# Overlapping the stages of MOE 1 in a single-core mLSTM and two-MOE kernel, with fewer warm-up products

## The chip, the cores and the metric

The kernel runs on one core of a Trainium2 chip. The metric is the device time of the core in microseconds (us): before the change it is 999.03 us, the median of three runs that lie between 998.11 and 1000.72 us. A core has a tensor engine (PE), a vector engine (DVE), a scalar engine (ACT), a general engine (POOL) and a queue that starts most transfers (SP); each runs its own list of instructions in the order in which it stands, and they wait for each other by semaphores.

## The reference

Three layers follow each other: a recurrent attention over 2 x 8 heads, a first MOE (a plain two-layer network with a piecewise activation), and a second MOE with eight experts whose gates are balanced over all tokens.

```
x = attn_out.transpose(0, 2, 1, 3).reshape(1536, 320)
# MOE 1
h = x @ w_in                       # 1536 x 320 @ 320 x 2048
g = where(h >= 1, h, where(h <= -1, 0, (h + 1) ** 2 / 4))
x = g @ w_out                      # 1536 x 2048 @ 2048 x 320
# MOE 2
P = exp(x @ w_gate - max); 8 times: P /= P.sum(1); P /= P.sum(0); P *= N / E
out = sum over e of P[:, e] * (relu(x @ w1[e]) @ w2[e])
```

## The kernel before

Large products are made in float32 split into a high and a low part, so that one product of the mathematics is eight matmuls of the chip. The tokens stand in twelve tiles of 128. Attention handles one tile after the other (`attn`, lines 370 to 465); its result goes, transposed and split, into `XH` and `XL`, which MOE 1 reads.

MOE 1 runs in five stages (`STAGES`, line 40): tokens 0 to 511 with the first half of the hidden layer, in two parts of 256 columns (stage 0); tokens 512 to 1023 with the first half (stage 1); tokens 1024 to 1535 with both halves (stage 2); then the second half for the first 512 (stage 3) and for the second 512 tokens (stage 4). The loop at line 587 goes over them. For each block of hidden units it makes a *first product* (`gemm_k`, line 131: eight matmuls into one of two PSUM banks named `g1`), an activation (`moe1_act`, lines 552 to 561: three operations on ACT, a maximum on DVE at line 558 that also releases the bank in the stages with 512 columns, a copy on ACT at 559, a subtraction on DVE at 560), and a *weighted sum* (`moe1_g2`, lines 563 to 574: eight matmuls with `w_out`, added up in three banks named `g2`). The sums are held back: `prevs` keeps up to three blocks (two in stage 0), so that a block's activation runs beside the products of the next ones.

At the end of a stage the loop at line 650 empties `prevs`, and only then the stage's accumulated banks are read: stages 0 and 1 copy them to memory (line 657), stages 2 to 4 add what was kept, fold the third bank and split the result into `XH` and `XL` (lines 659 to 666). All stages use the same three `g2` banks.

While stages 0 and 1 run, the loop calls `next(rest)` for pieces of the attention of tiles 2 to 11, and `pump_w` for decoding the weights of MOE 1 from 64-bit floats on ACT and DVE. A scheduler that works through the program at build time decides in which order each engine's instructions stand, so pieces of attention, first products and sums are mixed there.

`warm` (line 307) issues products of zeros that change no result: four ahead of the attention product of line 413 in tiles 2 to 7 (line 410), two ahead of each of the eight first products of stage 0 (line 615), and others at the start. PSUM has eight banks here: two `g1`, three `g2`, two `at` and one `ax`; `at` and `ax` serve attention, and after MOE 1 the gates of MOE 2 (`at`) and the fourth accumulator of MOE 2 (`ax`).

Of the kernel before, what the change touches and what calls it, by code (L numbers as in the profile page):

```python
# [12 lines left out]
ACTF = mybir.ActivationFunctionType  # L13
ALU = mybir.AluOpType
# [26 lines left out]
NPIECE = (9, 12, 18, 18, 18)  # L41
# [8 lines left out]
def mlstm_moe_moe_kernel(  # L50
# [14 lines left out]
    mm = nc.tensor.matmul  # L65
    act = nc.scalar.activation
    vec = nc.vector
# [8 lines left out]
    def bank(tag):  # L76
        n = {"g1": 2, "g2": 3, "at": 2, "ax": 1}[tag]
        return ps.tile([128, 512], F32, name="bk_" + tag, tag=tag, bufs=n)
# [20 lines left out]
    def htile(w, kind):  # L99

        if kind != "gs" and hhome:
            hcount[0] += kind == "hi"
            h = hhome[0][kind == "lo"]
            i = hcount[0] % (h.shape[1] // 512) * 512
            return h[:, i : i + w]
        n = {"gs": NGS, "hi": NHL, "lo": NHL}[kind]
        return pools["hp"].tile([128, 512], F32 if kind == "gs" else F32R, name=kind, tag=kind, bufs=n)[:, :w]
# [11 lines left out]
    def split_x(planes, cols):  # L119
        for k, x in planes:  # L120
            act(out=XH[:, k, cols], in_=x, func=ACTF.Copy)
        for k, x in planes:
            vec.tensor_tensor(out=XL[:, k, cols], in0=x, in1=f(XH[:, k, cols]), op=ALU.subtract)
# [9 lines left out]
    with ExitStack() as atx:  # L133
# [53 lines left out]
        wz = ap.tile([128, 128], mybir.dt.bfloat16, name="wz")  # L187
# [182 lines left out]
        def attn(t, tags):  # L370
# [29 lines left out]
            if not last:  # L400
                gp.tensor_tensor(
                    out=kw.rearrange("p (i r) d -> p r i d", r=2)[:, :, :, 0:40], in0=kk.rearrange("p (i r) d -> p r i d", r=2),
                    in1=G[:, :, 127:128].rearrange("p (r i) d -> p r i d", r=2).to_broadcast([128, 2, 4, 40]), op=ALU.mult,
# [3 lines left out]
                for pr in range(4):  # L407
                    mm(pi[:, pr * 82 : (pr + 1) * 82], qk_t[0:104, 0, pr, :], Cst[:, b, pr, :], start=True, stop=True)
            pa = bank(ta)
            if 2 <= t < 8:  # L410
                warm(WA, pa)
            for h in range(8):
                mm(pa[:, h * 41 : (h + 1) * 41], A[h % 2][:, h // 2, :], vw[:, h, :], start=True, stop=True)  # L413
# [3 lines left out]
            if not last:  # L417
# [6 lines left out]
                if c:  # L424
                    gp.tensor_tensor(
                        out=Cst[:, b, :, :], in0=Cst[:, b, :, :],
                        in1=lend[:, c * 8 + b * 4 : c * 8 + b * 4 + 4].unsqueeze(2).to_broadcast([104, 4, 82]), op=ALU.mult,
                    )
            pav = pa[:, 0:328].rearrange("p (h d) -> p h d", h=8)
            if c:  # L430
                hv = ap.tile([128, 8, 41], F32, name="hv", tag="hv")
                vec.tensor_tensor(
                    out=hv, in0=pi[:, 0:328].rearrange("p (h d) -> p h d", h=8),
# [118 lines left out]
        def moe1_act(pg, early):  # L552
            t, hi, lo = (htile(512, x) for x in ("gs", "hi", "lo"))
            act(out=t, in_=pg, func=ACTF.Relu, scale=-1.0, bias=1.0)  # L554
            act(out=t, in_=t, func=ACTF.Relu, scale=-0.5, bias=1.0)
            act(out=t, in_=t, func=ACTF.Square)  # L556
            g = pg if early else t
            dve_at.append(vec.tensor_tensor(out=g, in0=pg, in1=t, op=ALU.max))  # L558
            act(out=hi, in_=g, func=ACTF.Copy)
            vec.tensor_tensor(out=lo, in0=g, in1=f(hi), op=ALU.subtract)  # L560
            return hi, lo

        def moe1_g2(pp, first, last, f0, w, hi, lo):

            for u in range(512 // w):
                ff, ts = f0 + u, slice(u * w, u * w + w)
                wf = WM[ff // 8][1][:, ff % 8, :]
                st, sp = first, last and u == 512 // w - 1
                for k in range(2):
                    mm(pp[k], wf[:, k * 128 : (k + 1) * 128], hi[:, ts], start=st, stop=False)  # L570
                    mm(pp[k], wf[:, k * 128 : (k + 1) * 128], lo[:, ts], start=False, stop=False)  # L571
                    mm(pp[k], wf[:, 256 + k * 128 : 256 + (k + 1) * 128], hi[:, ts], start=False, stop=sp)  # L572
                mm(pp[2], wf[:, 512:640], hi[:, ts], start=st, stop=False)  # L573
                mm(pp[2], wf[:, 512:640], lo[:, ts], start=False, stop=sp)  # L574
# [9 lines left out]
        held = ap.tile([128, 3, 512], F32, name="held")  # L584
        g0f = G0.rearrange("p h t -> p (h t)")
        held = {0: [held[:, k, :] for k in range(3)], 512: [g0f[:, 0:512], g0f[:, 512:1024], id4]}
        for si, (t0, hfs, w) in enumerate(STAGES):
            nf = 512 // w
            f_last = hfs[-1] * 8 + 7
            pp = [bank("g2") for _ in range(3)]  # L590
            if w < 512:
                for p in pp:
                    mm(p, wz, wz[:, 0:1].to_broadcast([128, 512]), start=True, stop=False)
            prevs = []
            for hf in hfs:
                if si == 2 and hf == 0:

                    hhome[0] = [ap.tile([128, 1536], F32R, name=f"hq{i}", tag=f"qk{i}", bufs=1) for i in range(2)]
                if si == 3:
                    while w_state[0] < 18:  # L600
                        pump_w()
                    rtx.close()
                    rtx = ExitStack()
                    open_right(rtx, hp=1, raw=2, gw=1)
                    wgr = pools["gw"].tile([128, 3, NE], F32, name="wgr")
                    wgs = pools["gw"].tile([128, 5, NE], F32R, name="wgs")
                    wg2 = pools["gw"].tile([128, 2, 2, NE], F32R, name="wg2")
                    hhome.clear()
                for o in range(0, 512, w):
                    while len(done) * 128 < t0 + o + w:  # L610
                        next(rest)
                    for ff in range(hf * 8, hf * 8 + 8, nf):
                        need_w(ff + nf - 1)
                        pg = bank("g1")
                        if w < 512:
                            warm(WG, pg)
                        for u in range(nf):
                            fc = (ff + u) % 8 * 128
                            pe_at = gemm_k(pg[:, u * w : u * w + w], WM[hf][0], slice(fc, fc + 128), slice(t0 + o, t0 + o + w))
                        while len(prevs) >= (LAG2 if w == 512 else LAG1):  # L620
                            moe1_g2(*prevs.pop(0))
                        st = ff == hfs[0] * 8 and w == 512
                        sp = ff + nf - 1 == f_last and o + w == 512
                        prevs.append(([p[:, o : o + w] for p in pp], st, sp, ff, w, *moe1_act(pg, w < 512)))
                        if w_state[0] < NPIECE[si]:
                            if si:
                                with tc.issue_after(dve_at[-2].ins):
                                    pump_w()
                            else:
                                pump_w()  # L630
                        credit += nf * RATE[si]
                        while credit >= 1:
                            if si:

                                with tc.issue_after(pe_at[0].ins), tc.issue_after(dve_at[-3].ins):
                                    next(rest, None)
                            else:
                                next(rest, None)
                            credit -= 1
                        if si == 3 and ff == 12:  # L640
                            nc.sync.dma_start(wgr, w_gate)
                            split_k(wgs, 0, NE, wgr)
                            act(out=wg2.rearrange("p k u e -> p u k e"), in_=f(wgs[:, 0:4, :]).rearrange("p (u k) e -> p u k e", u=2), func=ACTF.Copy)
                            cur, jobs = expert_w(0)
                        if si * 8 + ff % 8 >= 28:
                            next(jobs, None)
            if si == 4:
                for _ in jobs:
                    pass
            for p in prevs:  # L650
                moe1_g2(*p)
            if si < 2:
                if si == 1:
                    for _ in rest:
                        pass
                for k, p in enumerate(pp):
                    act(out=held[t0][k], in_=p, func=ACTF.Copy)
                continue
            if si > 2:
                for k, p in enumerate(pp):  # L660
                    vec.tensor_tensor(out=p, in0=p, in1=held[t0][k], op=ALU.add)
            tr = htile(512, "gs")
            act(out=tr[0:64], in_=pp[2][64:128], func=ACTF.Copy)
            act(out=tr[64:128], in_=pp[2][0:64], func=ACTF.Copy)
            vec.tensor_tensor(out=tr, in0=pp[2], in1=tr, op=ALU.add)
            split_x([(0, pp[0]), (1, pp[1]), (2, tr)], slice(t0, t0 + 512))
        atx.close()


# [156 lines left out]
```

## Time and profile before

| what | value |
|---|---|
| time, median of 3 runs | 999.03 us (998.11 to 1000.72) |
| time of the profiled execution | 997.13 us |
| its span, first to last instruction | 995.1 us |
| PE busy | 978.6 us of the span, 98% |
| DVE busy | 472.1 us, 47% |
| ACT busy | 345.5 us, 35% |
| granted clock of PE | 1.00 of full speed (2.4 GHz) |
| MOE 2 begins | about 296 us after the span's start |

A row of the timeline gives the start, the duration, the engine, the line of the code and what is written and read; in brackets stands how long the engine was idle just before, and what it waited for. A matmul's duration includes its way through the array, and the next one starts before it ends, so the cost of one in a row of many is the distance between two starts. Times count from the start of the span.

### The profile page before, as it was taken

What the parts mean: (1) busy time and instruction counts of PE and PEld (TensorE: products, weight loads), DVE (VectorE), ACT (ScalarE), POOL (GpSimd) and SP (SyncE); (2) the same over time, 40 slices, a digit from 0 to 9 for tenths busy, and PEclk for the clock granted to TensorE, in tenths of its full rate; (3) what the DMA queues carried; (4) which work ended last, traced back from release to release, by engine and by line L of the source; (5) the groups of instructions that cost most, each with busy time, mean ns of one, the idle gap of its engine ahead of it and who ended that gap; (6) DMA issues with size and microseconds to landing.
All of it is one profiled execution on the core that took longest, in us unless ns stands there. A gap on an engine that the chain in (4) does not pass through costs nothing.

```text
span 995.1 us, 13508 instructions
## 1 busy us (share of the span) xinstructions
PE 978.6 (98%) x5520; PEld 860.2 (86%) x5520; DVE 472.1 (47%) x856; ACT 345.5 (35%) x625; POOL 32.2 (3%) x43
## 2 busy tenths in 40 slices
PE   9989999998999999999999999999999999999998
PEld 5778988787788899999999999999999999999997
DVE  9999796864454554322522432242253234222222
ACT  3643455886664223212411321141132113111111
POOL 2212110000000000000000000000000000000000
PEclk9999999999999999999999999999999999999999
DMA  6855430230002001200300210030021002000000
GB/s 171 260 171 164 123 111 2 82 115 2 1 30 88 1 1 58 59 1 2 117 1 1 68 49 1 1 117 1 1 85 34 1 16 72 1 1 1 27 27 27
DMA packets 42190, 51.91 MB, mean 52 GB/s; under 512 B 3360, under 2 KB 35744, under 8 KB 42128
## 3 DMA queue, kind: packets, MB, share of 16 engines
q1 hardware_dynamic: 42128, 51.05, 17.2%
q8 instruction: 43, 0.70, 0.3%
q14 instruction: 19, 0.16, 0.0%
HBM read 49.03 MB, written 2.01 MB: 51 GB/s over the span
## 4 chain that ended last, share of the span: by engine, by line
PE 88%; DVE 8%; ACT 2%; issue 1%; DMA 1%; DVEq 0%
PE bk_g L131 43%; PE bk_g L726 8%; PE bk_g L728 8%; PE bk_g L727 8%; PE bk_ax L727 3%; PE bk_ax L726 3%; PE bk_ax L728 3%; PE bk_g L570 2%; PE bk_g L572 2%; PE bk_g L571 2%; PE bk_at L413 2%; PE bk_at L392 1%; PE bk_g L574 1%; PE bk_g L573 1%; DVE G L396 1%
## 5 line engine op out<-in xcount | busy, mean ns | idle before, releaser
L131 PE MATMUL bk_g<-XH,wk 128*128 128x512 f32 (+1 forms) x1240 | 400.1, 388 | 4.2 <-DVE gs L558 4.2
L746 DVE SCALAR_TENSOR_TENSOR lo<-bk_g,hi 128x512 fp32r<-128x512 f32 x192 | 132.6, 691 | 375.8 <-ACT hi L745 374.9
L131 PE MATMUL bk_g<-XL,wk 128*128 128x512 f32 (+1 forms) x744 | 285.2, 384 | 0.0
L131 PEld LDWEIGHTS bk_g<-XH,wk 128*128 128x128 f32 x1240 | 230.6, 188 | 48.3 <-DVE gs L558 5.8
L745 ACT ACTIVATE hi<-bk_g 128x512 fp32r<-128x512 f32 x192 | 114.4, 596 | 455.0 <-PE bk_g L131 454.6
L726 PE MATMUL bk_g<-wf,hi 128*128 128x320 f32 x576 | 177.4, 308 | 0.0
L727 PE MATMUL bk_g<-wf,hi 128*128 128x320 f32 x576 | 177.0, 307 | 0.0
L728 PE MATMUL bk_g<-wf,lo 128*128 128x320 f32 x576 | 176.9, 308 | 0.0
L131 PEld LDWEIGHTS bk_g<-XL,wk 128*128 128x128 f32 x744 | 140.0, 188 | 21.9 <-issue 0.2
L726 PEld LDWEIGHTS bk_g<-wf,hi 128*128 128x128 f32 x576 | 108.0, 187 | 6.8 <-ACT hi L745 0.2
L727 PEld LDWEIGHTS bk_g<-wf,hi 128*128 128x128 f32 x576 | 108.1, 188 | 6.3
L728 PEld LDWEIGHTS bk_g<-wf,lo 128*128 128x128 f32 x576 | 107.9, 187 | 0.0
L727 PE MATMUL bk_ax<-wf,hi 128*128 128x320 f32 x192 | 59.1, 308 | 0.0
L726 PE MATMUL bk_ax<-wf,hi 128*128 128x320 f32 x192 | 59.0, 307 | 0.0
L728 PE MATMUL bk_ax<-wf,lo 128*128 128x320 f32 x192 | 58.4, 304 | 0.0
L554 ACT ACTIVATE gs<-bk_g 128x512 f32<-128x512 f32 x48 | 28.4, 592 | 36.1 <-PE bk_g L131 35.6
L558 DVE TENSOR_TENSOR gs<-bk_g,gs 128x512 f32<-128x512 f32 x40 | 27.4, 688 | 25.3 <-ACT gs L556 25.2
L760 DVE SCALAR_TENSOR_TENSOR acc<-bk_g,P,acc 128x320 f32<-128x320 f32 x63 | 30.8, 545 | 15.4 <-PE bk_g L728 15.4
L726 PEld LDWEIGHTS bk_ax<-wf,hi 128*128 128x128 f32 x192 | 36.1, 188 | 0.0
L728 PEld LDWEIGHTS bk_ax<-wf,lo 128*128 128x128 f32 x192 | 36.1, 188 | 0.0
L727 PEld LDWEIGHTS bk_ax<-wf,hi 128*128 128x128 f32 x192 | 35.9, 187 | 0.0
L544 DVE TENSOR_TENSOR wf<-raw,wf 128x640 fp32r<-128x640 f32 x32 | 26.4, 825 | 18.9 <-ACT wf L543 18.9
(214 smaller groups left out, 1001.0 us busy)
## 6 DMA issues: line engine op xcount, KB each, us to landing
raw<-in_w_dram SPq DMA_DIRECT2D x32, 320.0 KB
raw<-in_w_dram SPq DMA_DIRECT2D x32, 256.0 KB
kvo_t<-in_kvo_dram SPq DMA_DIRECT2D x12, 484.0 KB
raw<-in_w_out_dram SPq DMA_DIRECT2D x8, 640.0 KB
raw<-in_w_in_dram SPq DMA_DIRECT2D x8, 512.0 KB
raw<-in_w_dram SPq DMA_DIRECT2D x64, 64.0 KB
qk<-in_qk_dram SPq DMA_DIRECT2D x24, 160.0 KB
G<-g_d SPq DMA_DIRECT2D x5, 512.0 KB
```

The source lines that it names most:

```text
L131: return [mm(dst, a, b, start=i == 0, stop=i == len(seq) - 1) for i, (a, b) in enumerate(seq)]
L413: mm(pa[:, h * 41 : (h + 1) * 41], A[h % 2][:, h // 2, :], vw[:, h, :], start=True, stop=True)
L544: vec.tensor_tensor(out=wf[:, fs, 320:640], in0=rs[n], in1=f(wf[:, fs, 0:320]), op=ALU.subtract)
L554: act(out=t, in_=pg, func=ACTF.Relu, scale=-1.0, bias=1.0)
L558: dve_at.append(vec.tensor_tensor(out=g, in0=pg, in1=t, op=ALU.max))
L570: mm(pp[k], wf[:, k * 128 : (k + 1) * 128], hi[:, ts], start=st, stop=False)
L726: mm(pp[i], hi[:, ts], wf[:, ff, 0:320], start=st, stop=False)
L727: mm(pp[i], hi[:, ts], wf[:, ff, 320:640], start=False, stop=False)
L728: mm(pp[i], lo[:, ts], wf[:, ff, 0:320], start=False, stop=sp)
L745: act(out=hi, in_=pg, func=ACTF.Relu)
L746: vec.scalar_tensor_tensor(out=lo, in0=pg, scalar=0.0, in1=f(hi), op0=ALU.max, op1=ALU.subtract)
L760: vec.scalar_tensor_tensor(out=acc[:, t, :], in0=pp[i], scalar=P[:, t, e : e + 1], in1=acc[:, t, :], op0=ALU.mult, op1=ALU.add)
```

## The change

Three things change. First, the list `prevs` now lives across the stages. At the end of a stage it is not emptied: the last sums of a stage (three, two in stage 0) follow the first products of the next stage, one behind each, and the stage's banks are read (`moe1_end`) once its last sum is issued. Only stage 4 empties the list. Second, the accumulators are taken when a stage's first sum is issued, and stages 2 and 4 take the banks `ax`, `at`, `at` where stages 0, 1 and 3 take the three `g2`. The decoding of weights pauses in stage 2 while sums of stage 1 are still held back. Third, `warm` is called ahead of line 413 in tiles 2 to 4 in place of 2 to 7, and in stage 0 ahead of the first four first products in place of all eight: 12 and 8 products of zeros fewer.

```diff
-            if 2 <= t < 8:
+            if 2 <= t < 5:
                 warm(WA, pa)
...
+        prevs, ends = [], []
+        def run_prev():
+            stage, o, w, ff, st, sp, hi, lo = prevs.pop(0)
+            if not stage["pp"]:
+                stage["pp"] = [bank(x) for x in (("ax", "at", "at") if stage["id"][0] in (2, 4) else ("g2",) * 3)]
+                for p in stage["pp"] if w < 512 else ():
+                    mm(p, wz, wz[:, 0:1].to_broadcast([128, 512]), start=True, stop=False)
+            moe1_g2([p[:, o : o + w] for p in stage["pp"]], st, sp, ff, w, hi, lo)
+            if sp:
+                ends.append((*stage["id"], stage["pp"]))
+        def moe1_end(si, t0, pp):
+            if si < 2:
+                for k, p in enumerate(pp):
+                    act(out=held[t0][k], in_=p, func=ACTF.Copy)
+                return
+            if si > 2:
+                for k, p in enumerate(pp):
+                    vec.tensor_tensor(out=p, in0=p, in1=held[t0][k], op=ALU.add)
+            tr = htile(512, "gs")
...
         for si, (t0, hfs, w) in enumerate(STAGES):
...
-            pp = [bank("g2") for _ in range(3)]
-            if w < 512:
-                for p in pp:
-                    mm(p, wz, wz[:, 0:1].to_broadcast([128, 512]), start=True, stop=False)
-            prevs = []
+            stage = {"id": (si, t0), "pp": None}
...
-                        if w < 512:
+                        if w < 512 and o == 0:
                             warm(WG, pg)
...
                         while len(prevs) >= (LAG2 if w == 512 else LAG1):
-                            moe1_g2(*prevs.pop(0))
+                            run_prev()
...
-                        if w_state[0] < NPIECE[si]:
+                        prevs.append((stage, o, w, ff, st, sp, *moe1_act(pg, w < 512)))
+                        while ends:
+                            moe1_end(*ends.pop())
+                        if w_state[0] < NPIECE[si] and (si != 2 or prevs[0][0] is stage):
...
-            for p in prevs:
-                moe1_g2(*p)
...
+        while prevs:
+            run_prev()
+        moe1_end(*ends.pop())
```

On PE, at the border from stage 2 to stage 3, the kernel before has the last sums of stage 2 (lines 570 to 574, accumulators `bk_g2`), and then first products (line 131) into one `g1` bank after the other:

```order
L573 MATMUL bk_g2_1717<-hq0_1718,wf_1744 128x512
L574 MATMUL bk_g2_1717<-hq1_1719,wf_1744 128x512
L131 MATMUL bk_g1_2189<-XH_66,wk_634 128x512
L131 MATMUL bk_g1_2189<-XL_67,wk_634 128x512
L131 MATMUL bk_g1_2189<-XH_66,wk_634 128x512 x2
L131 MATMUL bk_g1_2189<-XL_67,wk_634 128x512
L131 MATMUL bk_g1_2189<-XH_66,wk_634 128x512 x2
L131 MATMUL bk_g1_2189<-XL_67,wk_634 128x512
L131 MATMUL bk_g1_2207<-XH_66,wk_634 128x512
L131 MATMUL bk_g1_2207<-XL_67,wk_634 128x512
L131 MATMUL bk_g1_2207<-XH_66,wk_634 128x512 x2
L131 MATMUL bk_g1_2207<-XL_67,wk_634 128x512
```

Now, where stage 3's own sums begin, the engine has one sum between every two first products, as inside a stage, and stage 2 was added up in `bk_ax` and `bk_at`:

```order
L573 MATMUL bk_at_1769<-hq0_1668,wf_1753 128x512
L574 MATMUL bk_at_1769<-hq1_1669,wf_1753 128x512
L131 MATMUL bk_g1_2220<-XH_66,wk_628 128x512
L131 MATMUL bk_g1_2220<-XL_67,wk_628 128x512
L131 MATMUL bk_g1_2220<-XH_66,wk_628 128x512 x2
L131 MATMUL bk_g1_2220<-XL_67,wk_628 128x512
L131 MATMUL bk_g1_2220<-XH_66,wk_628 128x512 x2
L131 MATMUL bk_g1_2220<-XL_67,wk_628 128x512
L570 MATMUL bk_g2_2229<-hi_2150,wf_1753 128x512
L571 MATMUL bk_g2_2229<-lo_2151,wf_1753 128x512
```

Four first products in a row became one, and three sums moved behind the first three. The same holds at the border from stage 3 to stage 4.

On PE, in the attention of tile 5, the kernel before has the last of four pairs of a load and a product of zeros ahead of line 413, and then parts of a first product of stage 0:

```order
L309 LDWEIGHTS wz_92
L309 MATMUL bk_at_923<-wz_92 128x512
L413 MATMUL bk_at_923<-vw_843,A_906 128x41
L131 MATMUL bk_g1_962<-XL_67,wk_89 128x256
L131 MATMUL bk_g1_962<-XH_66,wk_89 128x256
L408 MATMUL bk_ax_918<-Cst_115,qk1_96 128x82 x4
```

Now the four pairs are gone, and sums that stood further back come behind the first matmul of line 413:

```order
L131 MATMUL bk_g1_956<-XH_66,wk_89 128x256
L131 MATMUL bk_g1_956<-XL_67,wk_89 128x256
L413 MATMUL bk_at_921<-vw_843,A_904 128x41
L571 MATMUL bk_g2_658<-wf_88,wf_90 128x256
L572 MATMUL bk_g2_658<-wf_88,wf_90 128x256
L571 MATMUL bk_g2_659<-wf_88,wf_90 128x256
L572 MATMUL bk_g2_659<-wf_88,wf_90 128x256
L574 MATMUL bk_g2_660<-wf_88,wf_90 128x256
```

In all, between the last matmul of line 459 for tile 4 and the second matmul of line 413 for tile 5 there stood 14 matmuls of MOE 1 and four of zeros; now 22 of MOE 1 stand there.

On ACT, at the border from stage 1 to stage 2, the kernel before has the three copies of the finished banks (line 657) and copies of decoded weights (lines 266 and 267) ahead of the activation of the new stage's first block (lines 554 to 556):

```order
L657 ACTIVATE G0_91<-bk_g2_1271 128x512
L657 ACTIVATE G0_91<-bk_g2_1272 128x512
L657 ACTIVATE id4_117<-bk_g2_1273 128x512
L266 ACTIVATE wf_1744<-raw_747 128x2x256
L267 ACTIVATE wf_1744<-raw_747 128x2x64
L266 ACTIVATE wf_1744<-raw_1290 128x2x256
L554 ACTIVATE gs_1729<-bk_g1_1720 128x512
L267 ACTIVATE wf_1744<-raw_1290 128x2x64
L555 ACTIVATE gs_1729<-gs_1729 128x512
L556 ACTIVATE gs_1729<-gs_1729 128x512
```

Now the first two blocks' activations are past, and the copies (line 604) and the decoded weights stand among those of the third and fourth block:

```order
L554 ACTIVATE gs_1735<-bk_g1_1718 128x512
L555 ACTIVATE gs_1735<-gs_1735 128x512
L604 ACTIVATE G0_91<-bk_g2_1449 128x512
L556 ACTIVATE gs_1735<-gs_1735 128x512
L604 ACTIVATE G0_91<-bk_g2_1450 128x512
L604 ACTIVATE id4_117<-bk_g2_1451 128x512
L266 ACTIVATE wf_1753<-raw_747 128x2x256
L559 ACTIVATE hq0_1668<-gs_1735 128x512
L267 ACTIVATE wf_1753<-raw_747 128x2x64
L554 ACTIVATE gs_1778<-bk_g1_1758 128x512
```

The work of the stage's end moved behind two and a half activations.

## Rows read from the trace of the kernel before

**Rows 1.** The page: busy time of each engine; granted clock in 40 slices, in tenths.

```profile
PE 978.6 (98%) x5520; PEld 860.2 (86%) x5520; DVE 472.1 (47%) x856; ACT 345.5 (35%) x625; POOL 32.2 (3%) x43
PEclk9999999999999999999999999999999999999999
```

**Rows 2.** Stretches: length, busy of PE, PEld, DVE, ACT, POOL (count); clock, DMA.

```profile
56.00:66.00 10.00, 8.63 (x72) 7.93 (x70) 9.95 (x16) 4.99 (x11) 2.28 (x3) 1.00 0.24 64
66.00:76.00 10.00, 8.50 (x62) 7.41 (x63) 9.91 (x23) 3.98 (x9) 1.85 (x2) 1.00 0.69 198
76.00:86.00 10.00, 9.26 (x75) 8.31 (x74) 9.12 (x18) 4.33 (x9) 1.67 (x3) 1.00 0.64 198
86.00:96.00 10.00, 9.30 (x75) 8.09 (x73) 9.26 (x18) 3.58 (x9) 3.68 (x4) 1.00 0.59 188
96.00:106.00 10.00, 10.00 (x88) 9.84 (x88) 8.99 (x20) 3.58 (x8) 2.16 (x3) 1.00 0.42 109
106.00:120.00 14.00, 13.07 (x110) 12.35 (x109) 11.50 (x22) 4.88 (x10) 2.51 (x3) 1.00 0.40 124
```

**Rows 3.** Waits of PE: for whom, us in total, times, longest.

```profile
PE bk_g L131 <- DVE gs L558: 4.2, 3, 3.0
```

**Rows 4.** Timeline of PE: first products after a wait, stages 2, 3 and 4.

```profile
175.57 0.50 PE L131 MATMUL bk_g<-XH,wk 128*128 128x512 f32 x1 [1.04 <-DVE gs L558]
...
238.29 0.50 PE L131 MATMUL bk_g<-XH,wk 128*128 128x512 f32 x1 [2.96 <-DVE gs L558]
...
269.81 0.50 PE L131 MATMUL bk_g<-XH,wk 128*128 128x512 f32 x1 [0.20 <-DVE gs L558]
```

**Rows 5.** Timeline of PE inside stage 3: a sum, a product, the next sum.

```profile
242.07 0.39 PE L570 MATMUL bk_g<-hi,wf 128*128 128x512 f32 x1
...
243.93 0.39 PE L131 MATMUL bk_g<-XH,wk 128*128 128x512 f32 x1
...
245.77 0.39 PE L570 MATMUL bk_g<-hi,wf 128*128 128x512 f32 x1
```

**Rows 6.** Timeline of ACT and DVE: stage 1's copies; first two activations of stage 3.

```profile
170.03 1.07 ACT L657 ACTIVATE G<-bk_g 128x512 f32<-128x512 f32 x2
...
235.86 1.14 ACT L555 ACTIVATE gs<-gs 128x512 f32<-128x512 f32 x2
236.90 1.14 ACT L556 ACTIVATE gs<-gs 128x512 f32<-128x512 f32 x2
...
237.55 1.29 DVE L558 TENSOR_TENSOR gs<-bk_g,gs 128x512 f32<-128x512 f32 x2 [2.38 <-ACT gs L556]
```

**Rows 7.** Products of zeros: by line (ns min/median/max); timeline of four and the next instruction.

```profile
L309 PE MATMUL bk_at<-wz x24: 376/378/390, 46.5 to 110.8; 128*128 128x512 bf16 x24
...
110.11 1.03 PE L309 MATMUL bk_at<-wz 128*128 128x512 bf16 x4
110.98 1.87 PE L413 MATMUL bk_at<-vw,A 128*128 128x41 f32 x16
```

**Rows 8.** Timeline of PE, 64 to 118 us: what it waited for.

```profile
66.76 0.51 PE L570 MATMUL bk_g<-wf 128*128 128x256 f32 x2 [1.91 <-ACT wf L559]
67.65 0.59 PE L309 MATMUL bk_g<-wz 128*128 128x512 bf16 x2 [0.27 <-DVE wf L560]
...
77.91 0.59 PE L309 MATMUL bk_g<-wz 128*128 128x512 bf16 x2 [0.74 <-DVE wf L560]
...
88.50 1.76 PE L413 MATMUL bk_at<-vw,A 128*128 128x41 f32 x14 [0.34 <-DVE A L398]
...
92.91 1.13 PE L392 MATMUL bk_at<-qk 104*128 104x128 f32 x8 [0.36 <-DVE Cst L453]
...
117.14 0.62 PE L459 MATMUL bk_ax<-cst,sg 128*128 128x128 f32 x3 [0.93 <-DVE sg L446]
```

**Rows 9.** End of stage 4: PE's next first product; DVE's reads of two finished banks.

```profile
295.91 0.39 PE L131 MATMUL bk_g<-XH,wk 128*128 128x512 f32 x1
...
296.93 1.36 DVE L123 TENSOR_TENSOR XL<-bk_g,XH 128x512 fp32r<-128x512 f32 x2
```

More of the change, by code (lines that the diff above doesn't have):

```diff
@@ L586, in mlstm_moe_moe_kernel @@
         held = {0: [held[:, k, :] for k in range(3)], 512: [g0f[:, 0:512], g0f[:, 512:1024], id4]}
+        prevs, ends = [], []
[17 more added lines that the diff above has]
+            tr = htile(512, "gs")
+            act(out=tr[0:64], in_=pp[2][64:128], func=ACTF.Copy)
+            act(out=tr[64:128], in_=pp[2][0:64], func=ACTF.Copy)
+            vec.tensor_tensor(out=tr, in0=pp[2], in1=tr, op=ALU.add)
+            split_x([(0, pp[0]), (1, pp[1]), (2, tr)], slice(t0, t0 + 512))
         for si, (t0, hfs, w) in enumerate(STAGES):
@@ L620, in mlstm_moe_moe_kernel @@
                         while len(prevs) >= (LAG2 if w == 512 else LAG1):
-                            moe1_g2(*prevs.pop(0))
+                            run_prev()
                         st = ff == hfs[0] * 8 and w == 512
                         sp = ff + nf - 1 == f_last and o + w == 512
-                        prevs.append(([p[:, o : o + w] for p in pp], st, sp, ff, w, *moe1_act(pg, w < 512)))
-                        if w_state[0] < NPIECE[si]:
+                        prevs.append((stage, o, w, ff, st, sp, *moe1_act(pg, w < 512)))
+                        while ends:
+                            moe1_end(*ends.pop())
+                        if w_state[0] < NPIECE[si] and (si != 2 or prevs[0][0] is stage):
                             if si:
@@ L646, in mlstm_moe_moe_kernel @@
                             next(jobs, None)
-            if si == 4:
-                for _ in jobs:
-                    pass
-            for p in prevs:
-                moe1_g2(*p)
[L652 to L666, printed above, removed]
+            if si == 1:
+                for _ in rest:
+                    pass
+        for _ in jobs:
+            pass
+        while prevs:
+            run_prev()
+        moe1_end(*ends.pop())
         atx.close()
```

## The prediction

> **What bounds the kernel now.** I read the page first: PE is busy for 98% of the span, DVE for 47%, ACT for 35%, and the granted clock is full in all 40 slices [rows 1]. So at most about 2% can be had without taking work off PE, and the question is where PE waits, and whether it or DVE sets the pace there. The stretches answer the second: from 56 to 76 us DVE is busy for 9.9 of 10 us twice, and PE for 8.6 and 8.5; from 76 us on PE has 9.3, 9.3, 10.0 of 10 and 13.1 of 14, and DVE falls to 9.1, 9.3, 9.0 and 11.5 [rows 2]. So up to about 78 us DVE sets the end, and after it PE, with DVE close behind. The list of waits then names the largest wait of PE: a first product (line 131) that waits for the maximum of line 558, 4.2 us in three places [rows 3]. The timeline puts the three on the borders that the change touches: 1.04 us in stage 2, 2.96 us in stage 3, 0.20 us in stage 4, each at the third first product [rows 4]. The reason is in the order: without a sum between them two first products take 2 x 1.84 us, fill both `g1` banks, and the next needs a bank that only line 558 releases. On the border to stage 3 the activations of both blocks come as pairs on ACT, and their maxima end near 238.8 us, the first of them just before PE goes on at 238.29 [rows 4, 6].
>
> **The borders.** The change puts a sum between any two first products there. A sum takes 1.86 us and a product 1.84 us [rows 5]. From the end of one first product to the need of its bank, two products later, there then lie two sums and one product, 5.56 us; what must fit in is three operations on ACT at 0.57 us each [rows 6] and one on DVE at 0.65 us, 2.4 us in all. That leaves over 3 us for whatever else stands in those queues.
>
> The stage's end is what else. It is no new work (the same copies, additions and splits), but it now stands among activations. The heaviest place is the border to stage 2, where decoded weights come on top. Counted from the end T of the third product: in ACT's new order L554, L555, a copy and L556 end at T + 2.3; two copies and L266 at T + 4.0; then L559, L554, L266, L555, L556 at 0.57 us and two short L267 (taken as 0.3 us each) at T + 7.5; the maximum of the fourth block ends near T + 8.1. Its bank is wanted by the sixth product, after three sums and two products: T + 9.3. So 1.2 us are left, and I cost this edit at nothing; without that cover each further half microsecond on ACT would be half a microsecond of PE. The two later borders have less on ACT and come out with about as much room. From stage 4 to MOE 2 nothing is overlapped, before or now. There the first gate product now needs an `at` bank that held stage 4's second sum; DVE reads the first two banks until 298.29 us, and PE gets there after one product (1.84 us) and three matmuls (0.69 us) behind 295.91 us, at 298.44 [rows 9]. That just fits.
>
> Taking other banks costs no instruction, and the three zeroing matmuls of stage 0 are as many as before. Bounds of this term: all 4.2 us come back, or, if the waits only move to the next products, none. I take 4.2, since 1.2 us remain at the tightest place.
>
> **The warm-up products.** Twenty are gone. The row of a product of zeros says 0.378 us, but four in a row take from 110.11 to 110.98 us, 0.218 us each [rows 7]; that distance is the price where PE sets the pace. Two of the twenty stood at 67.65 us, where DVE is the bound: worth nothing. The other 18 stand from 77.91 us on [rows 8]: 18 x 0.218 = 3.92 us.
>
> They also covered waits, so the question is whether these grow. PE waits at 88.50, 92.91 and 117.14 us for 0.34, 0.36 and 0.93 us, for attention's steps on DVE [rows 8]. By the order, ahead of the first of these there were 14 short matmuls of MOE 1 and four of zeros, and now 22: eight matmuls of 256 columns at about 0.115 us (half the 0.23 us of 512, [rows 5]) replace 0.87 us with 0.92, so this wait stays at about 0.3. Ahead of the second there are five such matmuls as before: 0.36. Between the product of line 420 and the third wait there are 20 now for 14, so 0.7 of the 0.93 us is filled. Together 0.75 us less waiting, and 4.67 us in all.
>
> DVE limits that. From 76 to 120 us it is busy for 38.9 of 44 us [rows 2], so 5.1 us is the most that this stretch can shrink by, and 4.67 would leave DVE 0.4 us of rest. Its list there is nearly the same as before, and its steps wait on PE's in turn, so it will not be packed that tight: between 4.67 and nothing I take 4.0 us, close to the upper end because the chain of single steps above comes out near it.
>
> **The sum.** 4.2 + 4.0 = 8.2 us. Behind 300 us the program is the same and PE has no wait to give back. Against the profiled execution: 997.13 - 8.2 = 988.9 us. That execution is 1.9 us under the median of the runs shown, so against the median: 999.03 - 8.2 = **990.8 us**.
>
> **Rivals.**
> *DVE takes the warm-up part.* If DVE's order, not PE, already sets the pace from 78 us on, the removed products turn into longer waits ahead of lines 413, 392 and 459, and only the borders are left: 999.0 - 4.2 = 994.8 us. For it: DVE is over 90% busy up to 96 us. Against it: PE is busy for all of 96 to 106 us, when DVE has 1.0 us of rest.
> *The border waits only move.* The end of a stage delays the activations behind it, and the fifth or sixth product waits instead: 4.0 us are left, 995.0 us. For it: at the border to stage 2 ten operations stand between two maxima, and the room is 1.2 us. Against it: at the other two nothing is that close.
> *It does nothing.* Both happen: 999 us.
> *The clock falls.* The warm-up products keep PE busy where it waits for DVE. If PE ran at 1.2 GHz for the stretch from 56 to 76 us, its 17.1 us of work, less 0.44 us removed, would take 33.4 us in place of the 20 that DVE needs: 13.4 us more, and with the 8.2 us gained 999.0 + 5.2 = 1004.2 us, slower. The point from which it decides is some 14 us of PE's work at the lower level, with the 2.9 us of rest between; half of that only eats the gain. Against it: the granted clock is 1.00 in the stretch with 1.91 us of rest at 66.76 us, and nine tenths or more in the slice with the 2.96 us before 238.29 us [rows 1, 2, 4, 8], where no product of zeros stands; and from 76 us on PE will be busier than before. The Trainium skill (TensorE: Matmul & The Clock Gate, "What's actually happening") speaks for this rival: throttled is the default state and activity is what releases it, so padding that is taken out can cost the clock; no row here shows the lower level, so by the trace the sum is 990.8 us, and by that rule, if it bites in that stretch, 1004.2 us.
>
> **How the numbers follow.** The forecast (a gain of 6 to 10 us) 0.58, DVE 0.20, moved border waits 0.10, nothing 0.05, the clock 0.07. A change of 0.3% is 3.0 us, about what a measurement of this kernel tells from none. Faster by more: all of the forecast and most of the next two, 0.83; within: the rest of these and the fourth, 0.10; slower: 0.07. The forecast's lower end is all warm-up price, all three waits and all border waits, 3.92 + 1.63 + 4.2 = 9.75 us, 989.3 us, less some 1 us for the spread of the runs: 988. The upper end takes in the two rivals that keep half, 995.0 us, and the same 1 us: 996. The forecast alone would be 988 to 993.
>
> **What would show it.** Right: the waits of PE have no first product behind line 558, or under 0.5 us of it; MOE 2's first product comes near 288 us, not at 295.91; the waits of PE from 78 us to the end of stage 0 add up to about 1 us; the clock stays at 1.00. Wrong: a row of PE waiting for line 558, or for a copy of line 604, after the third product of a stage (the border waits moved); waits for lines 398, 453 or 446 that add up to over 3 us, with DVE near 100% busy (DVE took it); a stretch below 1.00 (the clock). A longer wait of the gate product behind stage 4, for the `at` bank, would take up to 1 us off the sum.

## The result and the profile after

| | before | changed | ratio, 95% |
|---|---|---|---|
| median, four timed executions each | 999.08 us | 989.57 us | 0.991 (0.9893 to 0.9928) |
| range of these | 998.11 to 1000.72 | 988.35 to 991.88 | |
| profiled execution | 997.13 us, span 995.1 | 988.54 us, span 986.4 | |

The kernel became 9.5 us faster, 8.6 us between the two profiled executions. The forecast was a gain of 8.2 us and a median of 990.8 us.

The page of the changed kernel, its busy time and its granted clock, beside [rows 1]:

```profile
PE 974.3 (99%) x5493; PEld 858.1 (87%) x5500; DVE 472.5 (48%) x856; ACT 345.5 (35%) x625; POOL 30.8 (3%) x43
PEclk9999999999999999999999999999999999999999
```

PE's busy time fell by 4.3 us, the span by 8.7: about half is work left out, half is waiting that went away. The list of what PE waits for (for whom, us in total, times, longest) no longer has the row of [rows 3]; these are its largest:

```profile
PE bk_g L570 <- ACT wf L559: 2.6, 2, 1.9
PE bk_g L309 <- DVE wf L560: 1.0, 1, 1.0
PE bk_g L309 <- DVE wz L188: 1.0, 1, 1.0
PE bk_at L392 <- DVE Cst L453: 0.8, 2, 0.5
PE bk_g L131 <- DVE wf L560: 0.7, 1, 0.7
```

All of these lie in the part before 143 us. The border to stage 3 in PE's timeline (start, length; the instructions between are left out), where [rows 4] have the 2.96 us:

```profile
230.19 0.40 PE L570 MATMUL bk_ax<-hq,wf 128*128 128x512 f32 x1
...
232.06 0.40 PE L131 MATMUL bk_g<-XH,wk 128*128 128x512 f32 x1
...
233.91 0.39 PE L570 MATMUL bk_g<-hi,wf 128*128 128x512 f32 x1
...
235.77 0.39 PE L131 MATMUL bk_g<-XH,wk 128*128 128x512 f32 x1
```

A sum of stage 2 (into `bk_ax`), a product of stage 3, the first sum of stage 3, the next product: each starts 1.85 to 1.87 us after the one in front, so nothing waits. At the end of stage 4, beside [rows 9]:

```profile
285.77 0.39 PE L131 MATMUL bk_g<-XH,wk 128*128 128x512 f32 x1
...
288.29 0.63 PE L697 MATMUL bk_at<-XH,wg 128*16 128x512 f32 x2
288.75 0.62 PE L699 MATMUL bk_at<-XL,wgs 128*8 128x512 f32 x2
...
289.67 0.39 PE L131 MATMUL bk_g<-XH,wk 128*128 128x512 f32 x1
```

MOE 2's first product comes at 285.77 us, 10.1 us earlier than in [rows 9]. Some 1.4 us of that is only order: the gate products of 288.29 to 289.67 us now stand behind it. They wait for no bank. The stretches of stage 0, beside [rows 2] (length, busy of PE, PEld, DVE, ACT, POOL; clock, DMA):

```profile
66.00:76.00 10.00, 7.70 (x54) 6.58 (x56) 9.86 (x23) 3.99 (x10) 1.32 (x2) 1.00 0.69 204
76.00:86.00 10.00, 8.73 (x75) 8.23 (x73) 9.14 (x17) 4.27 (x9) 2.35 (x3) 1.00 0.65 202
86.00:96.00 10.00, 9.73 (x84) 9.20 (x83) 8.60 (x18) 3.65 (x10) 2.21 (x2) 1.00 0.45 138
96.00:106.00 10.00, 9.96 (x88) 9.76 (x88) 9.45 (x20) 4.48 (x11) 2.90 (x5) 1.00 0.49 135
106.00:120.00 14.00, 13.95 (x113) 13.07 (x111) 13.35 (x25) 6.47 (x13) 4.57 (x5) 1.00 0.57 170
```

Up to 76 us DVE is as full as before and PE has more rest: two products of zeros are gone there, and nothing came sooner (the wait of [rows 8] that ended at 66.76 us ends at 67.34). From 86 us on PE is the full one, and DVE's rest shrank: it is busy for 13.35 of 14 us in the last row, where it had 11.50. Of PE's waits of [rows 8], the one ahead of 78 us is the same (now in front of a product), and those of 0.36 and 0.93 us are gone. Behind 78 us stand one of 0.53 us that is new, one of 0.27 us in place of 0.34, and one of 0.26 us. PE's timeline, with what it waited for:

```profile
67.34 0.50 PE L570 MATMUL bk_g<-wf 128*128 128x256 f32 x2 [1.92 <-ACT wf L559]
...
78.49 0.39 PE L131 MATMUL bk_g<-XH,wk 128*128 128x256 f32 x1 [0.74 <-DVE wf L560]
83.77 1.13 PE L392 MATMUL bk_at<-qk 104*128 104x128 f32 x8 [0.53 <-DVE Cst L453]
89.75 1.76 PE L413 MATMUL bk_at<-vw,A 128*128 128x41 f32 x14 [0.27 <-DVE A L398]
...
138.44 1.13 PE L392 MATMUL bk_at<-qk 104*128 104x128 f32 x8 [0.26 <-DVE Cst L453]
```

### The profile page after: what moved, and what is told of

It reads as the page before. It is cut to its first block, busy times and chain, and to the rows that moved or that the text cites. A ratio compares the mean times of both kernels' runs of the same rounds, so it can differ in the third digit from the quotient of the medians.

```text
span 986.4 us, 13451 instructions
## 1 busy us (share of the span) xinstructions
PE 974.3 (99%) x5493; PEld 858.1 (87%) x5500; DVE 472.5 (48%) x856; ACT 345.5 (35%) x625; POOL 30.8 (3%) x43
## 4 chain that ended last, share of the span: by engine, by line
PE 90%; DVE 7%; issue 1%; DMA 1%; ACT 0%; DVEq 0%
PE bk_g L131 44%; PE bk_g L741 9%; PE bk_g L743 9%; PE bk_g L742 8%; PE bk_ax L742 3%; PE bk_ax L741 3%; PE bk_ax L743 3%; PE bk_at L413 2%; PE bk_at L392 1%; DVE G L396 1%; PE bk_g L572 1%; PE bk_g L571 1%; PE bk_g L570 1%; DMA raw<-in_w_in_dram 1%; DVE dv L227 1%
```

## The experiments

Each was timed beside the kernel before, in one of three series. Medians of the kernel before there: 999.85, 999.14 and 999.68 us. A saving is taken against the median of its own series.

**The whole change again**, in the first series.

> The change as it is, timed beside its parts. Theory A (the border waits come back in full, and each removed product of zeros from 78 us on is worth its 0.218 us): 8.9 us less than the kernel before, 0.991. Theory B (only the borders pay, the warm-up part goes to DVE): 4.2 us less, 0.996.

Measured: 989.43 us (988.24 to 990.66), ratio 0.9897 (0.9879 to 0.9915), a saving of 10.4 us.

**The borders alone.** The changed kernel with the warm-up products of before:

```
-            if 2 <= t < 5:
+            if 2 <= t < 8:
...
-                        if w < 512 and o == 0:
+                        if w < 512:
```

> The new borders and banks, with all products of zeros as before. Theory A: 4.2 us less than before (0.9958), no wait of a first product for line 558 from stage 2 on, and about 4.7 us more than the whole change. Theory B: the same time as the whole change.

Measured: 994.06 us (993.08 to 994.66), ratio 0.9941 (0.9925 to 0.9956), a saving of 5.8 us. PE waits nowhere for line 558, and the saving is more than the 4.2 us of waiting that [rows 3] have.

**The warm-up products alone.** The kernel before with the opposite two lines:

> The old borders, with the 20 products of zeros left out. Theory A: 4 to 4.7 us less than before (0.9955), the border waits of 4.2 us still there. Theory B: the same as before within 1 us. Theory C (the clock needs these products): a stretch of stage 0 below 1.00, and slower than before.

Measured: 995.75 us (994.2 to 997.19), ratio 0.9959 (0.9944 to 0.9974), a saving of 4.1 us. The two parts add up to 9.9 us beside the whole's 10.4, so neither covers the other. The rows of this kernel also show where the 1.6 us may lie by which the borders gave more than their waits. PE's timeline behind the long border wait:

```profile
234.37 0.50 PE L131 MATMUL bk_g<-XH,wk 128*128 128x512 f32 x1 [2.97 <-DVE gs L558]
234.71 0.39 PE L131 MATMUL bk_g<-XL,wk 128*128 128x512 f32 x1
234.94 0.90 PE L131 MATMUL bk_g<-XH,wk 128*128 128x512 f32 x2
235.64 0.63 PE L131 MATMUL bk_g<-XL,wk 128*128 128x512 f32 x1
236.06 1.05 PE L131 MATMUL bk_g<-XH,wk 128*128 128x512 f32 x2
236.92 0.63 PE L131 MATMUL bk_g<-XL,wk 128*128 128x512 f32 x1
...
239.75 0.39 PE L570 MATMUL bk_g<-hi,wf 128*128 128x512 f32 x1
```

The stretches around it, of the same execution:

```profile
226.00:230.00 4.00, 4.00 (x19) 3.25 (x18) 2.08 (x3) 2.49 (x5) 0.00 (x0) 1.00 0.01 2
230.00:234.00 4.00, 1.41 (x7) 0.83 (x5) 1.07 (x2) 3.56 (x7) 0.00 (x0) 1.00 0.00 0
234.00:238.00 4.00, 3.63 (x10) 2.88 (x11) 2.21 (x4) 1.76 (x4) 0.00 (x0) 0.64 0.00 0
238.00:242.00 4.00, 4.00 (x17) 3.23 (x17) 0.93 (x2) 3.47 (x7) 0.00 (x0) 0.93 0.01 2
```

PE waits 2.97 us, starts at the full clock, and from about 235 to 238 us its matmuls of 512 columns stand 0.42 us apart in place of 0.23: the clock is at its lower level. From the wait's end to the next sum it is 5.38 us (234.37 to 239.75 us), where before it is 3.78 (238.29 to 242.07, [rows 4, 5]); so such a wait costs 2.97 us and about 1.6 us more. The trace of the kernel without attention's products of tiles 5 to 7, further down, has the same: 2.97 us of waiting, a lower clock behind it, and 5.37 us from the wait's end at 236.30 us to the next sum at 241.67. The profiled execution of before has the same wait and no such stretch.

**No warm-up product at all** in attention and MOE 1 (the changed kernel with `WA, WG = 0, 0`):

> The whole change, and the last 20 products of zeros in stage 0 and attention (12 ahead of line 413 in tiles 2 to 4, 8 ahead of the first four first products) left out too. Theory A: these stand where DVE sets the end, so nothing comes of it: within 1 us of the whole change. Theory B' (every product of zeros is PE time): 20 x 0.218 = 4.4 us less than the whole change. Theory C: the granted clock falls in a stretch between 36 and 78 us, and the time rises by up to 13 us.

Measured: 989.51 us (988.53 to 990.81), ratio 0.9897 (0.988 to 0.9915): the time of the whole change. Net, the products that the change keeps are worth nothing; the two at 67.65 us stood in the same stretch, but no run takes them out alone. Yet the clock falls here. A wait of this kernel and the stretches around it:

```profile
66.29 0.60 PE L570 MATMUL bk_g<-wf 128*128 128x256 f32 x2 [3.42 <-ACT wf L559]
...
66.00:68.00 2.00, 0.93 (x4) 0.64 (x4) 2.00 (x5) 1.11 (x3) 0.00 (x0) 0.64 0.92 224
68.00:70.00 2.00, 2.00 (x10) 2.00 (x11) 1.94 (x8) 0.34 (x1) 0.00 (x0) 0.50 0.98 287
70.00:72.00 2.00, 2.00 (x11) 2.00 (x11) 1.86 (x4) 0.00 (x0) 1.15 (x1) 0.50 1.11 352
72.00:74.00 2.00, 2.00 (x14) 2.00 (x14) 1.64 (x4) 0.26 (x1) 0.00 (x0) 0.65 0.31 119
```

The same wait and stretches of the whole change in the first series, and the next wait behind them:

```profile
66.75 0.50 PE L570 MATMUL bk_g<-wf 128*128 128x256 f32 x2 [1.92 <-ACT wf L559]
...
78.85 0.39 PE L131 MATMUL bk_g<-XH,wk 128*128 128x256 f32 x1 [0.75 <-DVE wf L560]
...
66.00:68.00 2.00, 0.99 (x6) 0.79 (x7) 2.00 (x6) 1.83 (x4) 0.00 (x0) 1.00 0.92 229
68.00:70.00 2.00, 2.00 (x15) 2.00 (x14) 1.94 (x7) 0.10 (x1) 0.00 (x0) 0.70 1.07 290
70.00:72.00 2.00, 2.00 (x12) 2.00 (x11) 1.70 (x4) 0.00 (x0) 0.77 (x1) 0.50 1.06 324
72.00:74.00 2.00, 2.00 (x15) 1.60 (x14) 1.54 (x4) 0.60 (x2) 0.00 (x0) 0.95 0.32 120
```

In both the clock halves behind a wait of line 570 for line 559, of 3.42 us without the products and of 1.92 us with those that the change keeps, and it is low for longer without. DVE is busy for 1.94 of 2 us from 68 to 70 us in both. A slower PE there still costs something: from the wait's end at 66.75 us to the product at 78.85 us are 12.10 us, and 11.15 us in the first trace of the same kernel (67.34 to 78.49 us), where the clock stays at 1.00. The timed executions agree: in the two series the whole change took 988.24 to 988.54 us with a mean clock of 0.999 or 1.000, and 989.20 to 991.88 us with 0.997 or 0.998. None of the six executions without the products has more than 0.997, so the time that these products cost and the time that the lower clock costs without them may have come out even; no run separates the two.

**The border waits filled instead of taken away.** The kernel before, with

```
+                        if si in (2, 3) and ff == hfs[0] * 8 + 2 and hf == hfs[0]:
+                            warm(4 if si == 2 else 12, bank("at"))
```

> The kernel before, with sixteen products of zeros put ahead of the third first product of stages 2 and 3 (five at the first place, eleven at the second), into an attention bank that is free there; the waits for line 558 stay, but PE is busy in most of them. Sixteen at 0.218 us are 3.5 us, of which about 1.1 and 2.4 us fit into waits of 1.04 and 2.96 us. Theory C: the new borders gain 5.8 us, more than the 4.2 us of waiting, because in some executions the granted clock is halved for some microseconds behind the 2.96 us wait (the trace of the kernel with fewer warm-up products alone shows 0.64 in 234 to 238 us). Then the fill gives about 1 to 1.5 us back without any overlap: a median near 998.6 us beside 999.85, executions with a mean clock of 0.994 are gone, and the rows from 234 to 242 us show 1.00. Rival D: the extra 1.6 us come from the new order or the banks, not from the clock. Then the fill gives nothing back: 999.5 to 1000.2 us, with as many low mean clocks as before.

The code has four products at the first place and twelve at the second, not five and eleven.

Measured: 998.18 us (997.38 to 998.94, 12 executions), ratio 0.9988 (0.9977 to 0.9999). PE's timeline at the border to stage 3:

```profile
235.91 2.34 PE L309 MATMUL bk_at<-wz 128*128 128x512 bf16 x10
238.80 0.50 PE L131 MATMUL bk_g<-XH,wk 128*128 128x512 f32 x1 [0.56 <-DVE gs L558]
239.14 0.39 PE L131 MATMUL bk_g<-XL,wk 128*128 128x512 f32 x1
239.37 0.63 PE L131 MATMUL bk_g<-XH,wk 128*128 128x512 f32 x2
```

(The profile has ten of the twelve.) The product comes no sooner, and the kernel is still some 1 us faster at the median, though the interval begins at 0.1 us. The clock is at 1.00 in all rows from 226 to 246 us. What is gone is the upper tail: none of the 12 executions has a mean clock below 0.998, where 6 of the 23 of before beside them have 0.994 to 0.997 and 999.67 to 1002.44 us. This is what theory C said; for D, the missing tail is harder to explain than the median. Grouped by mean clock, the 48 executions of before in the three series are:

| mean clock | executions | us, lowest, median, highest |
|---|---|---|
| 1.000 | 5 | 996.58, 996.95, 997.31 |
| 0.998 | 23 | 997.24, 998.86, 1000.07 |
| 0.997 and 0.996 | 9 | 999.62, 1000.57, 1001.63 |
| 0.995 and less | 11 | 1000.76, 1001.84, 1003.51 |

**One set of banks.** The whole change, but

```
-                stage["pp"] = [bank(x) for x in (("ax", "at", "at") if stage["id"][0] in (2, 4) else ("g2",) * 3)]
+                stage["pp"] = [bank("g2") for _ in range(3)]
```

> The whole change, but every stage sums into the three g2 banks as before, so a stage's first sum has to wait until the stage in front of it has been copied or added out of them. Theory E: the alternating banks are needed. At the border to stage 2 the copies on ACT come early enough, at the two later borders the first sums wait for DVE's additions and splits of the stage in front: about 0.6 to 1 us and 1.7 us, together 2 to 2.5 us, 991.5 to 992 us beside 989.4 us. Rival F: the two sums and the product that stand between cover it: no wait of PE at line 570 for lines 604 to 612, 989.4 us.

Measured: 989.13 us (988.17 to 989.92), ratio 0.9897 (0.988 to 0.9914). PE is busy for all 135 us from 165 to 300 us, as with the alternating banks. Theory E, my own estimate, falls: the stage's end is out of the banks in time without them.

**Decoding through the border.** The whole change without the condition `and (si != 2 or prevs[0][0] is stage)`.

> The whole change without its added condition: weights of MOE 2 are decoded through the border to stage 2 as well, as before. Theory G, the prediction's 1.2 us of room at that border: two to three more operations of ACT at 0.57 us then stand between two maxima, the room is used up, and a first product waits for line 558 for 0.2 to 1 us near 178 us: 989.6 to 990.4 us beside 989.4. Rival H: the room is larger than worked out, no wait appears, 989.4 us.

Measured: 990.0 us (989.12 to 992.06), ratio 0.9911 (0.9893 to 0.9929). The sizes cannot be told from the whole change's, but the waits can: no first product waits for line 558, and PE is busy for 134.98 of the 135 us. G's wait does not come; the room at the border to stage 2 is more than 1.2 us. In the profiled execution the clock is also at its lower level from 82.0 to 85.4 us, with no wait of PE over 0.74 us since the one that ended at 67.51 us.

**Attention's warm-up products alone**, those of tiles 5 to 7 (the kernel before with `2 <= t < 5`):

> The kernel before with the four warm-up products ahead of attention's line 413 taken out of tiles 5 to 7 alone; the eight of MOE 1's second blocks stay. Theory A: PE sets the pace from 78 us on, each costs the 0.218 us of four in a row: 12 x 0.218 = 2.6 us, 997.2 us beside 999.85, and the rest of the 4.1 us belongs to the products of MOE 1. Rival B: DVE takes part of it; 0 to 1.5 us, 998.4 to 999.9 us.

Measured: 996.21 us (994.23 to 998.03, 12 executions), ratio 0.9967 (0.9955 to 0.998), a saving of 2.9 us beside the 2.6 us of 12 x 0.218. Theory A fits, rival B does not (the interval is 2.0 to 4.5 us); the six of MOE 1 behind 78 us are left with about the 1.2 us that is missing to 4.1 (1.3 by the same price).

**The overlap at one border, and at all but that one.** Lines put in ahead of each stage of the whole change; the first kernel overlaps at stage 3 alone, the second (with `si == 3`) everywhere else:

```
+            while si != 3 and prevs:
+                run_prev()
+            while ends:
+                moe1_end(*ends.pop())
             stage = {"id": (si, t0), "pp": None}
```

> The whole change, but with the overlap at the border to stage 3 alone; at the other borders the last sums come before the next stage's first products again. Both theories: the waits of 1.04 us in stage 2 and 0.20 us in stage 4 come back, 1.2 us, and some 0.3 us in front of stage 1: 990.7 to 991 us beside 989.4. Theory C says besides that the mean clocks stay as high as with the whole change (0.997 and more), since the 2.96 us wait is gone.

Measured: 991.54 us (990.94 to 993.9), ratio 0.9913 (0.9892 to 0.9933), 2.1 us above the whole change of the first series. The waits in its timeline:

```profile
171.00 0.50 PE L131 MATMUL bk_g<-XH,wk 128*128 128x512 f32 x1 [1.04 <-DVE gs L558]
...
262.07 0.50 PE L131 MATMUL bk_g<-XH,wk 128*128 128x512 f32 x1 [1.67 <-DVE gs L558]
```

The wait in stage 2 is back at its old size. The one in stage 4 is 1.67 us in place of the 0.20 of [rows 4]. The border itself is as long as before: from the first product of stage 4 to the third it is 5.48 us here (256.59 to 262.07) and 5.48 us in the kernel before (264.33 to 269.81). But there the gate products of MOE 2 fill 1.6 us of it, in front of the wait (267.98 to 269.61), and here these stand behind stage 4. So this border has 1.5 us more rest than its wait of 0.20 us tells, once the gate products stand elsewhere, and both theories forecast too little (1.2 us of waits; here are 2.7). The mean clocks of its six executions are 0.998 and 0.999.

> The whole change, but without the overlap at the border to stage 3. Both theories: the wait of 2.96 us comes back. Theory C: in some executions the clock is halved behind it, which costs up to 1.7 us more: a median of 993.2 to 994 us, mean clocks down to 0.994, and a wider spread, from 992.4 to 995. Rival D (the clock has nothing to do with that wait): 992.4 us with the spread and the mean clocks of the whole change, 0.997 and more.

Measured: 995.31 us (992.88 to 997.44, 8 executions), ratio 0.995 (0.993 to 0.9969). The wait is back with 2.96 us. The mean clocks go down to 0.993, seven of eight are 0.997 or less, and the spread is 4.6 us; so D's forecast failed. C has the direction and not the whole size: the median is 5.9 us above the whole change of the first series, more than the 2.96 us and the 1.7 us of C together. Nor does the profiled execution (994.44 us) show C at work: its clock is at 1.00 from 230 to 246 us, and the lower level stands elsewhere, from 47.0 to 50.4 and from 70.9 to 74.3 us. The first of these costs some 1.3 us (14.74 us between the waits of line 309 that end at 46.67 and 61.41 us, 13.47 us in the first trace of the change, from 46.38 to 59.85). Where the clock fell in the executions of 0.993 is not known, and the last 1.2 us of the median stay unexplained.

**The order alone.** The changed kernel with one set of banks, without the condition on decoding, and with `WA, WG = 0, 0`:

> What is left when the parts that the runs so far put at nothing are taken out of the change: sums follow the next stage's products as in the change, but all sums go into the g2 banks, weights are decoded through the border, and no warm-up product of attention or MOE 1 is left. Theory: 989.4 us, as with the whole change, within 0.6. Rival: these parts help one another (without the products of zeros the clock falls more often, and with one set of banks and the decoding the border has no room): 991 to 992 us.

Measured: 989.9 us (989.51 to 990.65), ratio 0.9895 (0.9874 to 0.9916): within half a microsecond of the whole change. Its mean clocks are 0.995 to 0.997, as those of the kernel without warm-up products above, and lower than those of the whole change. So the order gives the whole gain, net of what the lower clock costs and the missing products give back.

## Why the prediction was right, point by point

**The borders, 4.2 us.** The mechanism is right: between two first products a sum, and the three waits of [rows 4] are gone. As a price of waiting alone the 4.2 us are right too: the one execution of the borders alone with a mean clock of 1.000 took 993.08 us, 3.9 us under the 996.95 us of the five of before with that clock. Against the medians it was 5.8 us, and this is the term that was mis-sized. The step is the sum's last, "999.03 - 8.2". It carried the 1.9 us between the profiled execution and the median over unchanged, and they shrank to 1.0 us (988.54 and 989.57). In part this was the price of the same border: behind the 2.96 us wait the clock halves in some executions, at 1.6 us each time. Two of the four traces that have this wait show it, and the fill, which kept the wait and gave 0.96 us back, agrees. How often it happens is not known, and the kernel with that border alone as before lost more than it explains.

**The room of 1.2 us** at the border to stage 2 was worked out too small; the decoding that the change keeps away from there causes no wait. The conclusion, nothing, stands. The gate product found its bank free at 288.29 us, as worked out.

**The warm-up products, 4.0 us.** They gave 4.1 us alone, and 4.6 us on top of the borders (994.06 to 989.43), between the 4.0 taken and the 4.67 of the working. The price of 0.218 us is borne out by tiles 5 to 7 (2.9 beside 2.6 us). Valued at nothing were two products where DVE sets the end; this was not measured by itself, but those left there are worth nothing, net. The three waits from 83 to 143 us and one of 0.15 us add up to 1.2 us, where about 1 us was expected; they are not the ones that the working named, since 0.53 us came ahead of an earlier step and the 0.36 us went.

**The rivals.** DVE did not take the warm-up part, though it came near: it has 0.65 us of rest in the 14 from 106 us on. The border waits moved nowhere. Of the clock the prediction said that no row shows the lower level; that was true of one execution and not of the kernel. Inside the stretch that it names, from 66 to 74 us, the clock does halve in some executions. The price of 13.4 us was too large by far: the lower level lasts some 3 to 7 us in these rows, where 17 us of work were assumed, and costs about 1 us. The Trainium skill (TensorE: Matmul & The Clock Gate, "What's actually happening") has it that the chip throttles by default and activity lifts it. The runs agree: without products of zeros the wait of line 570 is longer (3.42 us against 1.92) and so is the low stretch behind it (0.50 in two rows of 2 us and 0.64 and 0.65 beside them, against 0.70, 0.50 and 0.95). What such a stretch cost depended on where it lay: about 1 us near 68 us, where DVE is busy nearly all the time, 1.6 us on the border to stage 3.

## What to carry to other kernels

In this kernel the gain came from putting work of the stage in front between the first steps of the next one where two buffers were all that stood between PE and a chain on other engines; the order gave all of the gain at the borders, more banks none. Padding that keeps PE busy paid only in the border waits (0.96 us), where PE sets the end and the clock fell behind the wait in some executions; where PE is full it cost its distance in a row, and where another engine sets the end it was worth nothing, net. When one profiled execution is below the median, ask what the others have that it has not: a wait may cost more in them than its row says.

## What was not expected of the hardware

The clock halves for some microseconds behind single waits of PE: behind 2.97 us at the border to stage 3 (spacing 0.42 us for 0.23, with the first matmuls after the wait still at the full clock) and behind 1.92 us near 67 us. It need not: the trace of before has waits of 1.91 and 2.96 us at the same places with the clock at 1.00, and near 67 us two traces of the changed kernel differ in this. A long wait is not needed either, as the stretch from 82.0 to 85.4 us in the kernel that decodes through the border shows. What picks the executions was not found. The mean clock of an execution tells it: 1.000 goes with 996.58 to 997.31 us, 0.995 and less with 1000.76 to 1003.51 us, so that a thousandth is worth some 0.9 us of this kernel, an estimate from the medians of these two groups.
